# Two places more for raw weight pieces in block one of an attention and two-layer kernel

## The chip, the core and the metric

The kernel runs on one core of a Trainium2 chip. The metric is the time of one execution on the device, in microseconds (us); the median of several runs counts. TensorE (PE) multiplies matrices, VectorE (DVE), ScalarE (ACT) and GpSimd (POOL) work on elements, and SyncE (SP) issues all loads and stores of this kernel.

## The reference

```
def _attn_ref(q, k, v):                       # 4 batches, 8 heads, 576 tokens, 64 wide
    q_d, k_d, v_d = means over 4 neighbouring tokens
    out_d = sm_attn(q_d, k_d, v_d)             # softmax attention over the 144 pooled tokens
    out_up = np.repeat(out_d, factor, axis=2)
    mask = np.abs(pos[:, None] - pos[None, :]) < factor
    out_local = softmax(where(mask, q k^T / 8, -1e9)) v
    return (out_up + out_local).astype(np.float32)

x = attention output as (2304, 512)
h = x @ w_in;  x = relu(h)^2 @ w_out           # layer one: 512 -> 2048 -> 512, weights in float64
h = x @ w_in;  out = (h * cos(h)) @ w_out      # layer two, the same shapes, weights of its own
```

Matrix products of this precision are made of three parts: the weight is split into a high part and a low part of TensorE's fast 32-bit type, and so is the activation, and high x high, high x low and low x high are added.

## The kernel before, in words

The tokens are worked on as 40 windows of about 58 tokens; two windows are a `pair`. Layer one takes them in five blocks of eight windows (460 or 464 tokens). In block j, a loop over the 16 weight pieces f (128 of the 2048 hidden units each) makes stage A (`stage_a`, L808: 12 matmuls into the bank `ps_h`, of which there is one, from `xh`, `xl` and the weight's `w1hi` and `loa`), then on ScalarE `gt` (L832, L833) and its high part `gh` (L820), on VectorE the low part `gl` (L826), and stage B (`stage_b1`, L891: 12 matmuls into four `acc` banks). Stage A of a piece runs ahead of stage B of the piece before it.

The weights come as float64 in raw pieces of 1 MB. `conv1(f)` loads a piece (`load_raw`, L650, a tile named `raw`, of which there are two), and `split` makes a 32-bit float of it: a Prelu on ScalarE (L667) into a tile `bits` (two of them), a clamp (L671) and a shift (L674) on VectorE, and a join of the lower word (L676), which reads `raw` for the last time. Then ScalarE writes the high part `w1hi` (L687; 16 tiles `hi0` to `hi15`, one for each piece, which stay) and VectorE the low parts `loa` and `lob` (L697), which are also stored to `lo_d` (L726) and loaded again by later blocks (L734). So each of the 16 pieces of block one is converted just ahead of its use. Later the second layer's pieces pass through the same two raw tiles (`conv2`).

Ahead of block one there is a first phase: attention of the first batch's first eight windows. Its q and k (8 tiles), pooled values and value bands lie in tiles of weight high parts that are not in use yet: `spare` is the list of free ones, `kept` three that the value bands and a part of the pooled values take (`early_v`), `need` and `done` take and give back. One of the two raw tiles also holds pooled values in this phase. During block one, attention for block two is done beside the matmuls: pooling of the next batch (`pool`, loads `pl` at L264 and L267, sums at L368, L373, L375), its four `down` steps (scores L413, weights by GpSimd L424, transposes L434, values L450), and four `pair` steps (mask and scores L546 and L565, exponentials L387 or L398, transposes L504, values L607, the sum `xt` L624, and `xh` and `xl` at L636 and L638). When a block ends, its four banks are copied to a tile `y` (L929 on ScalarE, L931 on VectorE) and stored.

The program is written as generators, advanced in turn by a loop. A scheduling layer then sorts the instructions of each engine by a model of time; within an engine they run in that order. Places are handed out as the program is written: `used` and `caps` count tiles, and a generator goes on when a count allows it.

Of the kernel before, what the change touches and what calls it, by code (L numbers as in the profile page):

```python
# [8 lines left out]
F32 = mybir.dt.float32  # L9
F32R = mybir.dt.float32r  # L10
BF16 = mybir.dt.bfloat16
U32 = mybir.dt.uint32
AF = mybir.ActivationFunctionType
ALU = mybir.AluOpType
# [4 lines left out]
P = 128  # L19
# [12 lines left out]
DM = H * D  # L32
DFF = 2048
NK = DM // P
NF = DFF // P
# [10 lines left out]
AHEAD = 3  # L46
# [11 lines left out]
TOP_SCALE = 2.0 ** -112  # L58
TOP_ALPHA = 2.0 ** 32
TOP_MAX = (2.0 - 2.0 ** -3 - 2.0 ** -23) * 2.0 ** 16 * TOP_SCALE  # L60
LO_RING = (("loa", AHEAD), ("lob", AHEAD + LAG))
SPREAD = ("qk0", "pl", "dpr", "dpt")
LENT = {"dpr": "vw", "dpt": "pl"}
PRODUCTS = ((5, 5), (0, 0), (3, 6), (1, 1), (4, 4), (2, 2), (6, 3))
RANK = {"down": 0, "pair": 1, "pool": 2, "conv1": 3, "conv2": 3}
# [27 lines left out]
def kernel(  # L93
# [11 lines left out]
    nc = tc.nc  # L105
    weights = {1: w1.bitcast(U32), 2: w2.bitcast(U32)}
# [4 lines left out]
    wp = ctx.enter_context(tc.tile_pool(name="wp", bufs=1, side="right"))  # L111
# [19 lines left out]
    for t, v in zip(magic, (MAGIC, -MAGIC)):  # L131
# [9 lines left out]
    caps = {  # L141
        "a": 3, "h": 1, "acc": 4, "qkw": 2, "vw": 2, "pr": 4, "pt": 5, "xt": 2, "qp": 1, "xd": 2, "vp": 1, "av": 3, "pl": 2, "raw": 2,
        "dpr": 2, "dpt": 1, "qk0": 0,
    }
    used = dict.fromkeys(caps, 0)
# [5 lines left out]
    def need(name, n=1):  # L151
        while early[0] and name in SPREAD:
            if name not in ("qk0", "pl") and used[name] < caps[name]:
                used[name] += 1
                held.setdefault(name, []).append(None)
                return
            if spare:
                held.setdefault(name, []).append(spare.pop(0))
                return
            other = LENT.get(name)  # L160
            if other and used[other] < caps[other]:
                used[other] += 1
                held.setdefault(name, []).append(other)
                return
            yield
        while used[name] + n > caps[name]:
            yield
        used[name] += n

    def done(name, n=1):  # L170
        f = taken[name].pop(0) if early[0] and name in SPREAD else None
        if f is None:
            used[name] -= n
        elif f in caps:
            used[f] -= n
        else:
            spare.append(f)

    spare = list(range(AHEAD, NF))
    kept = [spare.pop() for _ in range(W0[1] // 4 + 1)]  # L180
    held, taken = {}, {}

# [465 lines left out]
    def load_raw(layer, f):  # L648
        raw = rawp.tile([P, 2 * DM, 2], U32, tag="raw", name="raw")
        nc.sync.dma_start(out=raw.rearrange("p c w -> p (c w)"), in_=weights[layer][f])  # L650
        return raw

    def behind(*names):
        for name in names:
            if name in last:
                return tc.issue_after(last[name])
        return nullcontext()
# [2 lines left out]
        return tc.issue_after(last["pe"]) if follows and not early[0] else nullcontext()  # L660

    def split(raw, hi, los=None, sums=None, held_back=None):
        low, top = raw[:, :, 0], raw[:, :, 1]
        x = rawp.tile([P, 2 * DM], U32, tag="bits", name="bits")
        xv = x.bitcast(F32)
        with behind("hi", "xh", "exp"):
            nc.scalar.activation(out=xv, in_=top.bitcast(F32), func=AF.Prelu, scale=TOP_SCALE, alpha=TOP_ALPHA)  # L667
        while held_back and held_back(0):
            yield
        with behind("pr" if early[0] and not added[0] else "gl", "xl"):  # L670
            nc.vector.tensor_scalar(  # L671
                out=xv, in0=xv, scalar1=TOP_MAX, scalar2=-TOP_MAX * TOP_ALPHA, op0=ALU.min, op1=ALU.max
            )
        nc.vector.tensor_scalar(out=x, in0=x, scalar1=3, scalar2=None, op0=ALU.logical_shift_left)  # L674
        yield
        joined = nc.vector.scalar_tensor_tensor(  # L676
            out=x, in0=low, scalar=29, in1=x, op0=ALU.logical_shift_right, op1=ALU.bitwise_or
        )
        if held_back and added[0] and "joined" not in last:
            last["xl"] = last["joined"] = joined.ins  # L680
        if sums:
            yield from sums(xv)
        yield "read"
        while held_back and held_back(1):
            yield
        with behind("hi", "xh", "xd"):
            nc.scalar.activation(out=hi, in_=xv, func=AF.Copy)  # L687
        yield
        while held_back and held_back(2):
            yield  # L690
        if los is None:
            nc.gpsimd.tensor_tensor(out=xv, in0=xv, in1=hi.bitcast(F32), op=ALU.subtract)
        else:
            for k, lo in enumerate(los()):
                cs = slice(k * DM, (k + 1) * DM)
                with behind("xl") if held_back else nullcontext():
                    nc.vector.tensor_tensor(out=lo, in0=xv[:, cs], in1=hi[:, cs].bitcast(F32), op=ALU.subtract)  # L697
        return xv
# [2 lines left out]
    lo1 = {}  # L701
    
    def conv1(f, after=0):
        yield from need("raw")
        raw = load_raw(1, f)
        yield
        yield
        while len(ready) < after or len(scored) < 4:
            yield
        hi1[f] = wp.tile([P, 2 * DM], F32R, tag=f"hi{f}", name=f"w1hi{f}")  # L710
        los = []

        def ring():
            los.extend(lop.tile([P, DM], F32R, tag=t, name=t, bufs=n) for t, n in LO_RING)
            return los

        waits = {0: lambda k: (divided[0], len(downs), len(ready))[k] < (W0[1], HPAIR, 6)[k], 1: lambda k: len(ready) < W0[1],
                 2: lambda k: k == 0 and "joined" not in last}
        for said in split(raw, hi1[f], ring, held_back=waits.get(f) if early[0] else None):
            if said:  # L720
                done("raw")
            yield
            while f == 2 and said and now[0] < 1:
                yield
        for k, lo in enumerate(los):
            nc.sync.dma_start(out=lo_d[f][:, k * DM:(k + 1) * DM], in_=lo.bitcast(F32))  # L726
            lo1[0, f, k] = lo
# [9 lines left out]
    def conv2(u):  # L737
        p, odd = divmod(u, 2)
        yield from need("raw")
        raw = load_raw(2, u)  # L740
        yield
        yield
        hi = rawp.tile([P, 2 * DM], F32R, tag="shi", name="shi", bufs=1)
        n = 3 * HALF
        rest = raw.rearrange("p c w -> p (c w)")
        total, top = rest[:, :n].bitcast(F32), rest[:, 2 * DM:2 * DM + n].bitcast(F32R)

        def sums(x):
            b11, b12, b21, b22 = (x[:, k * HALF:(k + 1) * HALF] for k in range(4))
            t1, t2, t3 = (total[:, k * HALF:(k + 1) * HALF] for k in range(3))  # L750
            with behind("gl", "xl"):
                nc.vector.tensor_tensor(out=t3, in0=b22, in1=b12, op=ALU.add)
            nc.vector.tensor_tensor(out=t1, in0=b12, in1=b11, op=ALU.subtract)
            yield
            with behind("gl", "xl"):
                nc.vector.tensor_tensor(out=t2, in0=t3, in1=b11, op=ALU.subtract)
            nc.vector.tensor_tensor(out=b12, in0=b21, in1=t2, op=ALU.subtract)
            yield

        steps, lo = split(raw, hi, sums=sums if odd else None), None  # L760
        while True:
            try:
                said = next(steps)
            except StopIteration as end:
                lo = end.value
                break
            if said and not odd:
                done("raw")
            yield
        if not odd:  # L770
            nc.sync.dma_start(out=wi_d[p][:, :2 * DM], in_=hi.bitcast(F32))
            nc.sync.dma_start(out=wi_d[p][:, 2 * DM:], in_=lo)
            return
        m = NPROD * HALF
        nc.sync.dma_start(out=wo_d[p][:, :2 * DM], in_=hi.bitcast(F32))
        nc.sync.dma_start(out=wo_d[p][:, m:m + 2 * DM], in_=lo)
        with behind("relu", "xh", "exp"):
            nc.scalar.activation(out=top, in_=total, func=AF.Copy)
        yield
        nc.gpsimd.tensor_tensor(out=total, in0=total, in1=top.bitcast(F32), op=ALU.subtract)  # L780
        yield
        nc.sync.dma_start(out=wo_d[p][:, 2 * DM:m], in_=top.bitcast(F32))
        nc.sync.dma_start(out=wo_d[p][:, m + 2 * DM:], in_=total)
        done("raw")
# [354 lines left out]
    for i in range(n1):  # L1139
        j, f = divmod(i, NF)  # L1140
# [40 lines left out]
    for i in range(n2 + 4):  # L1181
        j, p = divmod(i, NP2)
# [107 lines left out]
```

## Time and profile before

| | |
|---|---|
| median of 3 runs | 915.63 us (914.12 to 920.59) |
| profiled execution | 917.37 us |
| its span, first to last instruction | 915.6 us |
| TensorE busy | 892.2 us, 97% |
| VectorE busy | 644.6 us, 70% |
| ScalarE busy | 572.9 us, 63% |
| data moved | 223.55 MB, mean 244 GB/s |
| mean granted TensorE clock | 0.992 of full speed |

The profiled execution's own time lies a little above its span, since it counts what lies around the first and the last instruction. Times inside the profile are counted from the span's start.

### The profile page before, as it was taken

What the parts mean: (1) busy time and instruction counts of PE and PEld (TensorE: products, weight loads), DVE (VectorE), ACT (ScalarE), POOL (GpSimd) and SP (SyncE); (2) the same over time, 40 slices, a digit from 0 to 9 for tenths busy, and PEclk for the clock granted to TensorE, in tenths of its full rate; (3) what the DMA queues carried; (4) which work ended last, traced back from release to release, by engine and by line L of the source; (5) the groups of instructions that cost most, each with busy time, mean ns of one, the idle gap of its engine ahead of it and who ended that gap; (6) DMA issues with size and microseconds to landing.
All of it is one profiled execution on the core that took longest, in us unless ns stands there. A gap on an engine that the chain in (4) does not pass through costs nothing.

```text
span 915.6 us, 17788 instructions
## 1 busy us (share of the span) xinstructions
PE 892.2 (97%) x6950; PEld 812.8 (89%) x6950; DVE 644.6 (70%) x1266; ACT 572.9 (63%) x1039; POOL 93.1 (10%) x79
## 2 busy tenths in 40 slices
PE   7888999999999999999999999999999999999997
PEld 5667788888887888888998999999999999999997
DVE  7989987655775657553311188888888887888786
ACT  5678875455644555454534477677777677777774
POOL 2002110122303312221200000000000000000000
PEclk9899999999999999999999999999999999999999
DMA  9498878957898666884897966665666656566663
GB/s 296 166 320 301 300 284 301 326 209 257 300 331 281 253 234 220 299 313 162 285 393 245 345 233 195 206 193 185 201 206 197 201 198 199 192 193 206 207 229 104
DMA packets 72903, 223.55 MB, mean 244 GB/s; under 512 B 9620, under 2 KB 14612, under 8 KB 68724
## 3 DMA queue, kind: packets, MB, share of 16 engines
q1 hardware_dynamic: 72820, 222.43, 71.2%
q8 instruction: 54, 0.88, 0.4%
q14 instruction: 29, 0.24, 0.1%
HBM read 181.50 MB, written 40.89 MB: 243 GB/s over the span
## 4 chain that ended last, share of the span: by engine, by line
PE 86%; DMA 6%; DVE 5%; ACT 2%; issue 0%; DVEq 0%; ACTq 0%; SPq 0%
PE ps_h L843 22%; PE acc L915 19%; PE ps_h L808 19%; PE acc L891 18%; DMA pl<-in_pool_v_dram 3%; DMA pl<-in_pool_qk_dram 2%; PE ps_warm L1028 1%; PE ps_a L607 1%; PE ps_a L413 1%; PE ps_a L450 1%; DMA raw<-in_w_dram 1%; PE ps_a L565 1%; PE acc L913 1%; DVE vp L375 1%; PE ps_a L434 1%; PE ps_a L504 1%
## 5 line engine op out<-in xcount | busy, mean ns | idle before, releaser
L826 DVE TENSOR_TENSOR gl<-gt,gh 128x460 fp32r<-128x460 f32 (+1 forms) x80 | 58.8, 735 | 147.7 <-ACT gh L820 86.8
L843 PE MATMUL ps_h<-x,w2hi 128*128 128x256 f32 x1152 | 160.0, 281 | 0.0
L843 PEld LDWEIGHTS ps_h<-x,w2hi 128*128 128x128 f32 x1152 | 146.9, 188 | 0.1
L915 PE MATMUL acc<-bl,gh 128*128 128x256 f32 x504 | 140.6, 280 | 0.0
L808 PE MATMUL ps_h<-xh,w1hi 128*128 128x460 f32 (+1 forms) x320 | 123.0, 385 | 7.2 <-ACT gt L832 4.3
L891 PE MATMUL acc<-gl,w1hi 128*128 128x460 f32 (+1 forms) x320 | 120.9, 378 | 1.5 <-DVE gl L826 1.5
L808 PE MATMUL ps_h<-xl,w1hi 128*128 128x460 f32 (+1 forms) x320 | 119.9, 375 | 0.0
L832 ACT ACTIVATE gt<-ps_h 128x460 f32<-128x460 f32 (+1 forms) x80 | 44.2, 553 | 105.3 <-PE ps_h L808 105.2
L891 PE MATMUL acc<-gh,w1hi 128*128 128x460 f32 (+1 forms) x320 | 107.1, 374 | 0.0
L891 PE MATMUL acc<-gh,lo 128*128 128x460 f32 (+1 forms) x256 | 95.3, 372 | 0.0
L915 PEld LDWEIGHTS acc<-bl,gh 128*128 128x128 f32 x504 | 94.7, 188 | 0.0
L883 DVE TENSOR_TENSOR gl<-g,gh 128x896 fp32r<-128x896 f32 x72 | 78.2, 1086 | 11.0 <-ACT gh L878 11.0
L851 ACT ACTIVATE u<-ps_h,quarter 128x512 f32<-128x512 f32 x72 | 49.4, 686 | 52.2 <-PE ps_h L843 52.1
L915 PE MATMUL acc<-w2hi,gh 128*128 128x256 f32 x288 | 80.7, 280 | 0.0
L915 PE MATMUL acc<-w2hi,gl 128*128 128x256 f32 x288 | 80.2, 280 | 0.0
L858 DVE SCALAR_TENSOR_TENSOR r<-u,ps_h 128x512 f32<-128x512 f32 x72 | 49.4, 687 | 41.2 <-ACT u L853 40.4
L808 PEld LDWEIGHTS ps_h<-xh,w1hi 128*128 128x128 f32 x320 | 60.4, 189 | 17.0 <-ACT gt L832 5.0
L878 ACT ACTIVATE gh<-g 128x896 fp32r<-128x896 f32 x72 | 68.1, 946 | 10.4 <-DVE g L876 10.4
L863 ACT ACTIVATE r<-r,half_pi 128x512 f32<-128x512 f32 x72 | 51.8, 719 | 34.5 <-DVE r L859 34.5
L843 PE MATMUL ps_h<-x,w2lo 128*128 128x256 f32 x432 | 68.5, 280 | 0.0
L891 PEld LDWEIGHTS acc<-gl,w1hi 128*128 128x128 f32 x320 | 60.1, 188 | 9.2 <-DVE gl L826 2.6
L808 PE MATMUL ps_h<-xh,lo 128*128 128x460 f32 (+1 forms) x256 | 66.1, 377 | 0.0
(147 smaller groups left out, 1895.4 us busy)
## 6 DMA issues: line engine op xcount, KB each, us to landing
bl<-wo_d SPq DMA_DIRECT2D x70, 896.0 KB
raw<-in_w_dram SPq DMA_DIRECT2D x32, 1024.0 KB
lo<-lo_d SPq DMA_DIRECT2D x128, 256.0 KB
qkw<-in_win_qk_dram SPq DMA_DIRECT2D x16, 512.0 KB
pl<-in_pool_qk_dram SPq DMA_DIRECT2D x24, 288.0 KB
wo_d<-raw SPq DMA_DIRECT2D x16, 384.0 KB
out_dram<-o SPq DMA_DIRECT2D x18, 256.0 KB
vw<-in_win_v_dram SPq DMA_DIRECT2D x16, 256.0 KB
```

The source lines that it names most:

```text
L375: nc.vector.tensor_reduce(out=vp[:, i[0]:i[-1] + 1, hp * P:(hp + 1) * P], in_=t.rearrange("p (k j r) -> p k j r", k=len(i), r=FACTOR), op= ...
L808: nc.tensor.matmul(h[:, :n], a[:, c * P:(c + 1) * P], x[:, c, :n], start=i == 0, stop=i == len(order) - 1)
L826: last["gl"] = nc.vector.tensor_tensor(out=gl, in0=gt, in1=gh.bitcast(F32), op=ALU.subtract).ins
L832: last["relu"] = nc.scalar.activation(out=gt, in_=h, func=AF.Relu).ins
L843: nc.tensor.matmul(h[:, s * TB:(s + 1) * TB], a[:, c * P:(c + 1) * P], x[:, c], start=i == 0, stop=i == len(order) - 1,)
L851: nc.scalar.activation(out=u, in_=h, func=AF.Identity, bias=quarter, scale=float(1.0 / (2 * math.pi)))
L858: nc.vector.scalar_tensor_tensor(out=r, in0=u, scalar=-PI2_HI, in1=hv, op0=ALU.mult, op1=ALU.add)
L863: nc.scalar.activation(out=r, in_=r, func=AF.Sin, bias=half_pi, scale=1.0)
L878: nc.scalar.activation(out=gh, in_=g[:, 1:], func=AF.Copy)
L883: nc.vector.tensor_tensor(out=gl, in0=g[:, 1:], in1=gh.bitcast(F32), op=ALU.subtract)
L891: nc.tensor.matmul(acc[d][:, :n], a, x, start=f == 0 and i == 0, stop=f == NF - 1 and i == 2)
L915: nc.tensor.matmul(o, a[:, x], b, start=opens and i == 0, stop=p == NP2 - 1 and i == 2 and (k % 2 == 1 or k == NPROD - 1),)
```

## The change

Two pairs of high-part tiles, 12 to 15, become places for raw pieces in block one. `spare` is turned round, so that q and k of the first phase take the tiles 15 down to 8 (before: 3 to 10), and `kept` holds 3 to 5 (before: 15, 14, 13). When the first phase gives tiles 12 to 15 back, they go to a list `vacant` and not to `spare`. `conv1(f)` asks `raw_place` for a place: a raw tile if the count allows one, otherwise two vacant tiles of numbers above f. In the second case `load_spare` loads the piece as two halves of 512 KB. `split` works on a list of parts, so that the Prelu and the join run once for each half; the clamp, the shift and all later steps stay whole. After the join the two tiles return to `vacant`.

```diff
+NSPARE = 2
...
-            spare.append(f)
-
-    spare = list(range(AHEAD, NF))
+            (vacant if f >= NF - 2 * NSPARE else spare).append(f)
+
+    vacant = []
+    spare = list(range(NF - 1, AHEAD - 1, -1))
     kept = [spare.pop() for _ in range(W0[1] // 4 + 1)]
...
-        return raw
+        return [(slice(0, 2 * DM), raw)]
+
+    def load_spare(f, tags):
+        parts = []
+        for k, t in enumerate(tags):
+            cs = slice(k * DM, (k + 1) * DM)
+            raw = wp.tile([P, 2 * DM], F32R, tag=f"hi{t}", name="raw").bitcast(U32)
+            nc.sync.dma_start(out=raw, in_=weights[1][f][:, 2 * k * DM:2 * (k + 1) * DM])
+            parts.append((cs, raw.rearrange("p (c w) -> p c w", w=2)))
+        return parts
+
+    def raw_place(f):
+        while True:
+            if used["raw"] < caps["raw"]:
+                used["raw"] += 1
+                return ()
+            mine = [t for t in vacant if t > f]
+            if len(mine) > 1:
+                for t in mine[:2]:
+                    vacant.remove(t)
+                return mine[:2]
+            yield
...
-            nc.scalar.activation(out=xv, in_=top.bitcast(F32), func=AF.Prelu, scale=TOP_SCALE, alpha=TOP_ALPHA)
+            for cs, part in raw:
+                nc.scalar.activation(
+                    out=xv[:, cs], in_=part[:, :, 1].bitcast(F32), func=AF.Prelu, scale=TOP_SCALE, alpha=TOP_ALPHA
+                )
...
-        joined = nc.vector.scalar_tensor_tensor(
-            out=x, in0=low, scalar=29, in1=x, op0=ALU.logical_shift_right, op1=ALU.bitwise_or
-        )
+        for cs, part in raw:
+            joined = nc.vector.scalar_tensor_tensor(
+                out=x[:, cs], in0=part[:, :, 0], scalar=29, in1=x[:, cs], op0=ALU.logical_shift_right,
+                op1=ALU.bitwise_or,
+            )
...
-        yield from need("raw")
-        raw = load_raw(1, f)
+        tags = yield from raw_place(f)
+        raw = load_spare(f, tags) if tags else load_raw(1, f)
...
-            if said:
+            if said and tags:
+                vacant.extend(tags)
+            elif said:
                 done("raw")
```

Since the scheduling layer sorts anew, instructions move on every engine from the second piece of block one up to the first pieces of block two. Two places matter here.

SP's queue at the end of the first phase and the start of block one, before. Names are tiles; `raw` 128x2048 is a whole piece, `lo_d_99` and so on take the low parts of piece zero and the next ones.

```order
L513 DMA vw<-in_win_v_dram 128x512
L650 DMA raw<-in_w_dram 128x2048 x2
L726 DMA lo_d_99<-loa 128x512
L726 DMA lo_d_99<-lob 128x512
L650 DMA raw<-in_w_dram 128x2048
L524 DMA qkw<-in_win_qk_dram 128x1024
L264 DMA pl<-in_pool_qk_dram 128x576 x2
L726 DMA lo_d_100<-loa 128x512
L726 DMA lo_d_100<-lob 128x512
L650 DMA raw<-in_w_dram 128x2048
L264 DMA pl<-in_pool_qk_dram 128x576
```

The same place now, with the changed kernel's line numbers (L660 loads a half, L652 a whole piece, L755 stores low parts).

```order
L515 DMA vw<-in_win_v_dram 128x512
L660 DMA raw<-in_w_dram 128x1024 x4
L652 DMA raw<-in_w_dram 128x2048 x2
L755 DMA lo_d_99<-loa 128x512
L755 DMA lo_d_99<-lob 128x512
L660 DMA raw<-in_w_dram 128x1024 x2
L526 DMA qkw<-in_win_qk_dram 128x1024
L266 DMA pl<-in_pool_qk_dram 128x576 x2
L755 DMA lo_d_100<-loa 128x512
L755 DMA lo_d_100<-lob 128x512
L266 DMA pl<-in_pool_qk_dram 128x576 x2
```

Four halves (pieces one and two) and two whole pieces (three and four) stand ahead of the first low-part store, where two whole pieces (one and two) stood; piece five follows as halves. From piece six on every piece is loaded whole.

ScalarE's order where block one ends, before. `ps_h_2028` is stage A of block one's last piece, `ps_h_2123` that of block two's first one, `ps_h_2210` of its second; `acc_887` and `acc_889` are banks of block one's result.

```order
L636 ACTIVATE xh<-xt 128x4x112
L832 ACTIVATE gt<-ps_h_2028 128x460
L833 ACTIVATE gt<-gt 128x460
L820 ACTIVATE gh<-gt 128x460
L506 COPY pt<-ps_a 128x256
L371 COPY qp<-qc 64x144 x2
L398 ACTIVATE pr<-pr 128x256 x2
L832 ACTIVATE gt<-ps_h_2123 128x460
L833 ACTIVATE gt<-gt 128x460
L820 ACTIVATE gh<-gt 128x460
L929 COPY y<-acc_887 128x460
L929 COPY y<-acc_889 128x460
```

The same place now; `ps_h_2135` is block two's first stage A and `ps_h_2222` its second, `acc_903` and `acc_905` the banks.

```order
L638 ACTIVATE xh<-xt 128x4x116
L958 COPY y<-acc_903 128x460
L958 COPY y<-acc_905 128x460
L508 COPY pt<-ps_a 128x256
L638 ACTIVATE xh<-xt 128x4x112
L508 COPY pt<-ps_a 128x256
L400 ACTIVATE pr<-pr 128x256 x2
L861 ACTIVATE gt<-ps_h_2135 128x460
L862 ACTIVATE gt<-gt 128x460
L849 ACTIVATE gh<-gt 128x460
L861 ACTIVATE gt<-ps_h_2222 128x460
```

The copies of block one's result now stand ahead of the last `xh` of block two's input (128x4x112) and ahead of block two's first `gt`; before, they stood behind both. On VectorE the copies of the two other banks stand ahead of the last `xl` in the same way, and TensorE has all of block one's stage B ahead of block two's first stage A, and then block two's second stage A right behind the first.

## Rows read from the trace of the kernel before

**Rows 1.** The page, part 1: busy us of each engine (share of the span), instructions.

```profile
PE 892.2 (97%) x6950; PEld 812.8 (89%) x6950; DVE 644.6 (70%) x1266; ACT 572.9 (63%) x1039; POOL 93.1 (10%) x79
```

**Rows 2.** Busy time by stretch: its length, engines, granted clock, DMA share, GB/s.

```profile
32.00:36.00 4.00, 3.44 (x40) 2.70 (x40) 3.54 (x8) 1.82 (x6) 0.00 (x0) 1.00 0.00 0
42.00:52.00 10.00, 7.33 (x48) 5.47 (x48) 9.89 (x17) 4.80 (x9) 0.00 (x0) 1.00 0.60 205
48.00:105.00 57.00, 51.63 (x353) 40.99 (x354) 51.03 (x103) 44.09 (x127) 9.17 (x9) 1.00 0.90 316
105.00:160.00 55.00, 55.00 (x463) 46.00 (x461) 46.30 (x93) 38.89 (x89) 5.06 (x7) 1.00 0.85 295
```

**Rows 3.** SP's queue in order of time: start, duration, line, load.

```profile
27.70 8.33 SPq L650 DMA_DIRECT2D raw<-in_w_dram  x2
...
59.88 0.33 SPq L650 DMA_DIRECT2D raw<-in_w_dram  x1
```

**Rows 4.** ScalarE in order of time: three Prelus; in brackets idle before, and releaser.

```profile
43.96 1.18 ACT L667 ACTIVATE bits<-raw 128x1024 f32<-128x1024 f32 x1 [1.96 <-DVE lob L697]
...
51.56 1.15 ACT L667 ACTIVATE bits<-raw 128x1024 f32<-128x1024 f32 x1 [1.80 <-DMA raw<-in_w_dram]
...
67.03 1.13 ACT L667 ACTIVATE bits<-raw 128x1024 f32<-128x1024 f32 x1 [3.86 <-DMA raw<-in_w_dram]
```

**Rows 5.** TensorE's waits from 36 to 105 us: total us, times, longest.

```profile
PE ps_h L808 <- ACT gt L832: 2.3, 1, 2.3
PE ps_h L808 <- ACT w1hi L687: 1.7, 3, 1.0
PE acc L891 <- DVE gl L826: 1.5, 2, 0.9
PE ps_h L808 <- ACT xh L636: 1.1, 1, 1.1
PE ps_a L434 <- POOL dpr L424: 0.9, 1, 0.9
PE ps_a L413 <- ACT dpt L441: 0.5, 1, 0.5
PE ps_a L434 <- ACT dpr L387: 0.3, 1, 0.3
PE ps_a L450 <- ACT dpt L441: 0.2, 1, 0.2
```

**Rows 6.** VectorE in order of time: a join, a low part, a pooling sum.

```profile
45.25 1.23 DVE L676 SCALAR_TENSOR_TENSOR bits<-raw,bits 128x1024 uint32<-128x1024 uint32 x1
...
49.25 0.68 DVE L697 TENSOR_TENSOR loa<-bits,w1hi 128x512 fp32r<-128x512 f32 x1
...
54.84 0.75 DVE L368 TENSOR_REDUCE qc<-pl 128x144 f32<-128x576 f32 x1 [1.40 <-DMA pl<-in_pool_qk_dram]
```

**Rows 7.** Busy time by stretch, the first loads.

```profile
6.00:8.00 2.00, 2.00 (x9) 0.83 (x8) 1.08 (x2) 0.30 (x1) 0.00 (x0) 1.00 1.02 364
```

**Rows 8.** DMA issues: engine, count, KB of each.

```profile
qk<-in_pool_qk_dram SPq DMA_DIRECT2D x8, 288.0 KB
```

**Rows 9.** VectorE in order of time: the last xl of block two's input.

```profile
148.53 0.63 DVE L638 TENSOR_TENSOR xl<-xt,xh 128x448 fp32r<-128x448 f32 x1 [0.65 <-ACT xh L636]
```

**Rows 10.** The chain that ended last, around the end of block one.

```profile
150.06 0.22 PE ps_a L504 x2
...
150.99 2.71 PE ps_h L808 x12
153.69 4.59 PE acc L891 x22
```

**Rows 11.** The same chain after 281 us.

```profile
281.69 0.55 ACT gt L832
...
282.28 4.35 PE ps_h L808 x12
```

**Rows 12.** Busy time by stretch, the same place.

```profile
280.00:285.00 5.00, 3.02 (x11) 2.35 (x10) 4.11 (x11) 3.60 (x7) 2.18 (x2) 0.80 0.97 368
```

More of the change, by code (lines that the diff above doesn't have):

```diff
@@ L662, in split @@
     def split(raw, hi, los=None, sums=None, held_back=None):
-        low, top = raw[:, :, 0], raw[:, :, 1]
         x = rawp.tile([P, 2 * DM], U32, tag="bits", name="bits")
@@ L744, in conv2 @@
         n = 3 * HALF
-        rest = raw.rearrange("p c w -> p (c w)")
+        rest = raw[0][1].rearrange("p c w -> p (c w)")
         total, top = rest[:, :n].bitcast(F32), rest[:, 2 * DM:2 * DM + n].bitcast(F32R)
```

## The prediction

> **What bounds the kernel now.** I read the page's busy shares first, then the busy time by stretch, then the waits of TensorE, and last the engines behind these waits. TensorE is busy for 892.2 of 915.6 us [rows 1], so a change of loads can win at most the 23 us in which it is not, and only in the stretch where loads are late. From 105 to 160 us TensorE has no gap at all, while from 48 to 105 us, the first nine or ten pieces of block one, it is busy for 51.63 of 57.00 us [rows 2]: 5.37 us of idle time. This is the stretch of the change. In it the DMA engines are busy to 0.90, VectorE for 51.03 us, ScalarE for 44.09 us. Earlier, from 32 to 36 us, nothing is loaded at all (share 0.00) [rows 2].
>
> The queue shows why loads are late there. Pieces one and two (counted from zero) are issued in one row that begins at 27.70 us and lasts 8.33 us, to 36 us, because piece two has to wait until piece zero has been read; piece five is issued at 59.88 us, when piece three has been read [rows 3]. Its first reader, the Prelu of line 667, starts at 67.03 us, after ScalarE stood 3.86 us for this load; the Prelu at 51.56 us stood 1.80 us in the same way [rows 4]. But the Prelu at 43.96 us waited 1.96 us for VectorE's low part, through the two `bits` tiles [rows 4]: no weight load is late there.
>
> How much of this reaches TensorE is in its list of waits from 36 to 105 us [rows 5]. Two of them end before 48 us and have nothing to do with loads: 1.1 us for the block's input (xh) and 2.3 us for gt, the first block-one evacuation, which stands behind a conversion on ScalarE. After 48 us there are 1.7 us for w1hi (three waits), 1.5 us for gl (two: 0.9 and, by difference, 0.6), and 0.9 + 0.5 + 0.3 + 0.2 = 1.9 us for the pooled attention's steps. Together 5.1 of the 5.37 us.
>
> **The change, part by part.** *Two places more.* Pieces one and two no longer wait for a raw tile: their four halves are issued once the scores of the first phase are read, behind the last vw load of the first phase; piece three then takes the tile of the pooled values (27.70 us), piece four that of piece zero (36 us) [rows 3]. So by 40 us five pieces have been asked for, not three: 2 MB move out of the full stretch into one in which the engines stand still. At 316 GB/s [rows 2] that is 6.6 us of queue time fewer between 48 and 105 us. Piece five reuses the halves of piece one. From piece six on everything is in the two old places: the lead of two pieces passes on, but is not renewed from piece eight.
>
> *What goes.* The waits for w1hi, 1.7 us, are those behind late raw pieces and go. Of gl's 1.5 us, the longer one of 0.9, at the first gl, stays: VectorE has next to no gap before it, 9.89 of the 10 us from 42 to 52 [rows 2]. The other 0.6 goes: VectorE stood 1.40 us for a pooled piece at 54.84 us [rows 6], queued behind a raw load. The 1.9 us of the attention's steps come from a VectorE that runs late after such waits; I let them go as well. Sum: 1.7 + 0.6 + 1.9 = 4.2 us. Bounds: 1.7, if only weight waits go, and 5.37.
>
> *What halves cost.* Three pieces take two Prelus and two joins in place of one. A join of 1024 columns takes 1.23 us, an operation of 512 columns 0.68 us [rows 6], so two halves cost 2 x 0.68 - 1.23 = 0.13 us more. Pieces one and two lie in the stretch where VectorE has no gap: 0.26 us. Piece five hides behind TensorE's work. The Prelus hide in ScalarE's idle time there (12.9 of 57 us). SP issues three loads more; behind them stand the lo stores and the pool loads, and SP has gaps of microseconds between rows [rows 3]. The eight loads of q and k of 288 KB at the start moved 364 GB/s with the engines full [rows 7, 8], so I charge halves of 512 KB nothing. The Trainium skill ("DMA: Bandwidth & Descriptors", "Anatomy of one DMA — SWDGE (gpsimd) path") gives each transfer a fixed part of about 2.0 us beside its bytes, measured on another issue path; charged in full for piece five, whose second half falls into the full queue, the sum below would be 2.0 us worse, about -0.6 in place of -2.6 us; the row with 364 GB/s does not bear it out.
>
> *The order of first-phase tiles.* q and k take tiles 15 down to 8, the value bands and one pooled piece tiles 3 to 5. Their readers belong to the first phase, which is over when block one begins at 42 us; piece three, the first to take one of the three, is converted from 51.56 us on [rows 4]. No cost.
>
> *The end of block one.* The engines' order is made anew, and here is the price. On ScalarE the two copies of block one's result (y) now stand ahead of the last x of block two and ahead of the first gt of block two; before, one more gt stood between. Since these copies need the last matmuls of block one, block two's first matmul now starts only when block one is finished, with no rest of it left to fill. Before, the last xl was written at 148.53 us [rows 9], block two's first 12 matmuls ran at 150.99 us and 22 matmuls of block one (4.59 us) followed them as cover [rows 10]. Without it the chain of add, xh and xl, each taken at the 0.63 us of xl [rows 9], 1.9 us, is covered only by transposes and scores, 0.93 us (150.06 to 150.99) and two more transposes of 0.22 [rows 10]: 1.15 us. 0.75 us stay open. Then block two's second group waits for the single ps_h bank, an evacuation of 0.55 us [rows 11], with nothing beside it. Together 1.3 us. Bounds: 0, if attention is early, and 5.7, see the slower rival.
>
> *Sum.* -4.2 + 0.26 + 1.3 = -2.6 us. The profiled execution took 917.37 us, its span 915.6, so 1.8 us lie around it; the median of the three runs is 915.63 us, 0.2% below the profiled one. I take the difference to the median: 915.6 - 2.6 = 913.0 us.
>
> **The rivals.** *Slower: the drain at the end of block one costs the clock.* After 280 us TensorE stands for 2.0 us behind a late gt (busy 3.02 of 5.00 us), the granted clock has a mean of 0.80 there [rows 12], and the next 12 matmuls take 4.35 us [rows 11], against 2.71 us for the 12 at 150.99 us [rows 10]: 1.64 us more, at the lower level of 1.2 GHz for most of them. If attention for block two is not faster (its steps lie on VectorE and GpSimd and only partly behind loads), the drain becomes that case: 1.9 us uncovered, two groups of 12 at the low level (3.3 us), the evacuation 0.55: 5.7 us. With only the w1hi waits gone, -1.7 + 0.26 + 5.7 = +4.3, so 919.9 us. It decides when TensorE stands some 2 us there. For it: the new order itself. Against it: the 2.3 us wait near 46 us [rows 5] left the clock at 1.00 [rows 2], and pools and scores get their loads earlier too.
>
> *The change does not do what it says.* VectorE is the engine that delays TensorE, with 51.03 of 57 us busy, and early pieces just wait for it; the gain of 1.7 us goes into halves and drain. Change about 0, 915.5 us. For it: the `bits` wait at 43.96 us. Against: VectorE itself stood for loads [rows 6].
>
> *More gain.* All 5.37 us go and attention is early enough that nothing drains: 915.6 - 5.4 = 910.2. If then also the stall at 280 us is hit differently, since all transfers come earlier against it, its 2.0 + 1.64 us go: 906.6. For it: the stall hangs on loads of pooled values one after another. Against it: the order of instructions there is unchanged.
>
> **How the numbers follow.** Forecast, -1 to -4.5 us: 0.50, time 913.0. More gain: 0.20. No effect, within 1 us: 0.14. Slower rival: 0.16. A change under 1% (9.2 us) can hardly be told from none by these three runs, which spread from 914.12 to 920.59. The forecast, the rival without effect, most of the gains and nearly all of the losses lie inside it. The range goes from 908, the gain with part of the later stall, to 919.5, most of the slower rival: I leave out about 0.1 below and 0.07 above. Faster by over 1% needs nearly all of both gains: 0.06; slower by over 1% needs twice the slower rival's drain: 0.03; within 1%: 0.91.
>
> **What would show it.** In the changed profile the halves should be issued between 22 and 28 us and the DMA share of 32 to 36 us should be well above 0. The Prelus of pieces three and five should not wait for loads, and TensorE's w1hi waits between 48 and 105 us should be gone, its idle time there between 1 and 2 us; if they stay behind gl or dpr, VectorE is the bound. The waits of 2.3 and 1.1 us before 48 us should stand as they are. About 150 us a new gap of some 1.3 us should stand ahead of block two. If this gap is over 2 us and the granted clock there under 1.00, the slower rival holds. The forecast is wrong in its mechanism if TensorE's idle time of 48 to 105 us stays above 4 us, or if the time moves in stretches after 300 us.

## The result, and the profile after

The changed kernel takes 924.02 us (median of 12 runs, 919.80 to 929.34), the kernel before, beside it, 917.61 us (12 runs): a ratio of 1.0072 with an interval of 1.0048 to 1.0097, so 6.4 us slower, where 2.6 us less were forecast. The profiled executions lie further apart: 926.37 us with a span of 924.6 us, against 917.37 and 915.6.

The page of the changed kernel, part 1 (busy us, share, instructions), stands against [rows 1]:

```profile
PE 894.9 (97%) x6950; PEld 815.1 (88%) x6950; DVE 645.0 (70%) x1269; ACT 573.5 (62%) x1042; POOL 95.6 (10%) x79
```

TensorE stands for 924.6 - 894.9 = 29.7 us, before for 23.4: 6.3 of the 9.0 us of span. The other 2.7 us are matmuls that took longer. The busy time by stretch (columns as in [rows 2]) says where:

```profile
32.00:36.00 4.00, 3.00 (x34) 2.25 (x34) 3.90 (x10) 2.01 (x7) 0.00 (x0) 1.00 0.63 257
48.00:57.00 9.00, 8.20 (x31) 7.05 (x32) 6.10 (x13) 6.67 (x18) 0.00 (x0) 0.81 0.83 274
48.00:105.00 57.00, 48.37 (x310) 40.50 (x311) 48.20 (x98) 40.91 (x114) 6.04 (x7) 0.91 0.81 269
89.00:105.00 16.00, 11.67 (x80) 9.81 (x79) 11.78 (x27) 11.89 (x40) 3.09 (x3) 0.79 0.83 272
155.00:182.00 27.00, 24.88 (x268) 20.27 (x267) 14.55 (x33) 12.14 (x25) 1.19 (x2) 1.00 0.81 277
```

The loads do what the change says: from 32 to 36 us the DMA share is 0.63, not 0.00, and from 48 to 105 us it has fallen from 0.90 to 0.81 [rows 2]. Yet TensorE's idle time in that stretch has risen from 5.37 to 8.63 us, VectorE and ScalarE are less busy as well, and the granted clock has a mean of 0.91. (0.7 us of the rise is no new stop: the wait for gt, 2.3 us before and 2.4 us now, ends at 48.80 and not at 48.06 us, and so falls into the stretch.) From 155 to 182 us 2.12 us are idle, where TensorE had no gap at all before.

TensorE's waits from 36 to 105 us, against [rows 5]:

```profile
PE ps_a L548 <- ACT dpr L389: 3.7, 1, 3.7
PE ps_h L837 <- ACT gt L861: 2.4, 1, 2.4
PE ps_h L837 <- DVE loa L724: 1.9, 1, 1.9
PE ps_h L837 <- ACT xh L638: 1.2, 1, 1.2
PE acc L920 <- DVE gl L855: 1.0, 1, 1.0
PE ps_a L415 <- ACT pr L389: 0.5, 1, 0.5
PE ps_h L837 <- ACT w1hi L714: 0.4, 1, 0.4
```

The waits for w1hi are down from 1.7 to 0.4 us, as forecast. Two that were not there before, of 3.7 and 1.9 us, outweigh them. In this profile both lead to an instruction that waits for a load in front of work that was ready. VectorE in order of time, at the shorter one:

```profile
57.13 0.75 DVE L370 TENSOR_REDUCE qc<-pl 128x144 f32<-128x576 f32 x1 [3.03 <-DMA pl<-in_pool_qk_dram]
57.91 0.75 DVE L375 TENSOR_REDUCE kp<-pl 128x144 f32<-128x576 f32 x1
58.58 0.68 DVE L724 TENSOR_TENSOR loa<-bits,w1hi 128x512 fp32r<-128x512 f32 x1
```

A pooling sum stands 3.03 us for its load, and the low part of piece two, for which TensorE waits, is queued behind it. The old order has the same sum ahead of the same low part, and there TensorE does not wait for it. Before, the sum stood 1.40 us, at 54.84 us [rows 6], and the low part came next:

```profile
55.51 0.68 DVE L697 TENSOR_TENSOR loa<-bits,w1hi 128x512 fp32r<-128x512 f32 x1
```

New are the second sum between the two (0.67 us) and a load that came later. ScalarE in order of time, at the longer stop:

```profile
91.42 1.12 ACT L690 ACTIVATE bits<-raw 128x1024 f32<-128x1024 f32 x1 [4.50 <-DMA raw<-in_w_dram]
92.44 0.37 ACT L389 ACTIVATE dpr<-ps_a,dmx 96x144 f32<-96x144 f32 x1
```

The Prelu of piece eight, loaded into one of the two old places, stands 4.50 us for that load, and the exponentials of the pooled attention behind it hold a bank that TensorE's next scores need. SP issued the load at 82.92 us:

```profile
82.92 0.35 SPq L652 DMA_DIRECT2D raw<-in_w_dram  x1
```

What the stop does to the matmuls behind it (TensorE in order of time):

```profile
93.67 0.42 PE L548 MATMUL ps_a<-const_b 64*64 64x256 bf16 x2 [3.71 <-ACT dpr L389]
...
95.33 0.75 PE L837 MATMUL ps_h<-xh,w1hi 128*128 128x460 f32 x1
95.88 0.59 PE L837 MATMUL ps_h<-xl,w1hi 128*128 128x460 f32 x1
96.26 0.59 PE L837 MATMUL ps_h<-xh,w1hi 128*128 128x460 f32 x1
96.64 0.59 PE L837 MATMUL ps_h<-xl,w1hi 128*128 128x460 f32 x1
```

They follow each other after 0.38 us. At 85 us, ahead of the stop, the same matmuls did so after 0.21:

```profile
85.08 0.37 PE L837 MATMUL ps_h<-xl,w1hi 128*128 128x460 f32 x1
85.28 0.37 PE L837 MATMUL ps_h<-xh,w1hi 128*128 128x460 f32 x1
85.49 0.37 PE L837 MATMUL ps_h<-xl,w1hi 128*128 128x460 f32 x1
```

The granted clock is at its lower level, 1.2 of 2.4 GHz, from 93 to 100 us, and also from 49 to 52 us behind the wait of 2.4 us for gt.

Two readings are left. **Theory O:** the order is what costs. The scheduling layer has put many rows elsewhere (a row is one instruction in an engine's order), all between about 45 and 185 us, and engines that keep their order now stand in front of late loads with ready work behind. How many rows depends on the way of counting: the expectations below say some 550 matmul, 210 VectorE and 140 ScalarE rows; the fewest whose move turns one order into the other, by line and shape, are 141, 73 and 53. **Theory L:** the loads cost. A pooled load is queued behind the halves of piece five, and from piece six on the look-ahead is back at two places.

### The profile page after: what moved, and what is told of

It is laid out like the page before. It is cut to its first block, busy times and chain, and to the rows that moved or that the text cites. A ratio compares the mean times of both kernels' runs of the same rounds, so it can differ in the third digit from the quotient of the medians.

```text
span 924.6 us, 17794 instructions
## 1 busy us (share of the span) xinstructions
PE 894.9 (97%) x6950; PEld 815.1 (88%) x6950; DVE 645.0 (70%) x1269; ACT 573.5 (62%) x1042; POOL 95.6 (10%) x79
## 4 chain that ended last, share of the span: by engine, by line
PE 85%; DMA 7%; DVE 6%; ACT 2%; issue 0%; SPq 0%; DVEq 0%; ACTq 0%
PE ps_h L872 22%; PE acc L944 19%; PE ps_h L837 18%; PE acc L920 18%; DMA pl<-in_pool_v_dram 4%; DMA pl<-in_pool_qk_dram 2%; PE ps_warm L1057 1%; DMA raw<-in_w_dram 1%; PE ps_a L452 1%; PE ps_a L415 1%; PE ps_a L609 1%; PE ps_a L567 1%; PE ps_a L436 1%; PE acc L942 1%; DVE bits L702 1%; DVE vp L377 1%
## 5 line engine op out<-in xcount | busy, mean ns | idle before, releaser
L837 PEld LDWEIGHTS ps_h<-xl,w1hi 128*128 128x128 f32 x320 | 61.3, 192 | 7.7 <-DVE xl L640 1.6
```

Source lines behind the costliest of these rows:

```text
L837: nc.tensor.matmul(h[:, :n], a[:, c * P:(c + 1) * P], x[:, c, :n], start=i == 0, stop=i == len(order) - 1)
```

## The experiments

**Loads and order taken apart.** The order of all matmuls, VectorE and ScalarE instructions can be written out and tied, with edges that set the order alone. Each row is named by its line and its number among the rows of that line; the halves stand where the whole Prelu and join stood. Tied to its own order, the kernel before keeps every row in its place on every engine, so the tie itself moves nothing. SP's queue is not tied. In the two runs that follow it came out, but for the weight pieces and two other loads, as in the kernel whose order is tied, so "order" takes in the order of the pooled loads and of the low parts on SP. No run tells the two apart.

```diff
...
+    for name, said in ORDER.items():
+        chain = []
+        for run in said.split():
+            line, _, span = run.partition(":")
+            a, _, b = span.partition("-")
+            chain += [at[name, int(line), k] for k in range(int(a), int(b or a) + 1)]
+        for one, two in zip(chain, chain[1:]):
+            tc.add_manual_dep(
+                two, one.name, mybir.DependencyInfo(mybir.DependencyClass.NoSync, mybir.DependencyReason.DATA),
+                reason="the other kernel's order",
+            )
```

*New loads, old order:*

> The changed kernel with all its loads (two more places, halves, piece five in the halves of piece one), but the matmuls, the VectorE and the ScalarE instructions each stand in the order of the kernel before, tied by order-only edges. Theory O (the loss is the new order: between about 45 and 185 us some 550 matmul, 210 VectorE and 140 ScalarE rows stand elsewhere, and attention steps and weight steps get in each other's way): the loss of 6 to 9 us goes; time from 4 us below to 1 us above the kernel before, TensorE idle for at most 5.4 us from 48 to 105 us, no stop of 3.7 us at 90 us, no half clock after 48 us, and the forecast of -2.6 us can be seen or not. Theory L (the loss is the loads: a pooled load queued behind the halves, look-ahead back to two places from piece six): still 4 to 9 us slower than before, with stops behind a load.

Measured: 918.81 us beside 918.11, ratio 1.0006 (0.9987 to 1.0025). *Old loads, new order:*

> The kernel before with its loads, but matmuls, VectorE and ScalarE instructions in the order of the changed kernel. Theory O: 4 to 9 us slower than before, with stops of TensorE at about 57 and 90 us and a half clock behind them. Theory L: within 1.5 us of before. A third reading, that the new order is right for the new loads and wrong for the old ones, would show as more than 9 us.

Measured: 926.20 us beside 918.11, ratio 1.0088 (1.0057 to 1.0119). Old loads in the new order are as slow as the changed kernel, new loads in the old order as fast as the kernel before. Theory O is shown, with SP's order as part of it; L falls. (The third reading expected over 9 us; by the ratio it is 8.1, with 5.2 to 10.9 allowed, so a small share of it is not excluded.) The stretches agree. New loads, old order (48 to 105 us and 155 to 182 us; columns as above):

```profile
48.00:105.00 57.00, 53.33 (x358) 43.12 (x359) 52.78 (x109) 46.05 (x131) 9.97 (x9) 0.97 0.84 282
...
155.00:182.00 27.00, 27.00 (x221) 23.07 (x220) 16.15 (x33) 12.72 (x23) 3.70 (x5) 1.00 0.92 319
```

Old loads, new order:

```profile
48.00:105.00 57.00, 47.18 (x308) 39.08 (x308) 48.53 (x95) 40.13 (x112) 9.78 (x7) 0.94 0.85 291
105.00:155.00 50.00, 48.43 (x348) 38.93 (x347) 39.78 (x78) 35.12 (x87) 9.95 (x8) 1.00 0.84 279
155.00:182.00 27.00, 25.21 (x269) 20.57 (x268) 14.04 (x32) 12.16 (x26) 1.19 (x2) 1.00 0.83 280
```

In the first, the idle time of 48 to 105 us is 3.67 us, 1.7 less than before, and there is none at the end of block one. (Its clock is at the lower level from 49 to 52 us, and the waits of 1.5 us for gl that before has [rows 5] do not occur behind these longer matmuls; a run with the full clock there follows below.) In the second it is 9.82 us, more than in the changed kernel, and the stops around 160 to 180 us are there with the old loads too. The stops are not at the same places in all details (here TensorE waits 3.1 us for w1hi and 2.3 us for GpSimd's pr, not for loa and dpr): the new order meets whichever load is late.

**An order made anew without other loads.** Only pieces one, two and five are written in halves, with the old loads:

```diff
...
-            nc.scalar.activation(out=xv, in_=top.bitcast(F32), func=AF.Prelu, scale=TOP_SCALE, alpha=TOP_ALPHA)
+            for cs in cut:
+                nc.scalar.activation(
+                    out=xv[:, cs], in_=top[:, cs].bitcast(F32), func=AF.Prelu, scale=TOP_SCALE, alpha=TOP_ALPHA
+                )
...
+        cut = [slice(k * DM, (k + 1) * DM) for k in range(2)] if f in (1, 2, 5) else (slice(0, 2 * DM),)
```

The join likewise.

> The kernel before with its loads, in which only the Prelu and the joining instruction of pieces one, two and five are written as two halves each; the scheduler then moves some 345 matmul, 150 VectorE and 110 ScalarE rows of block one. Theory O: the time moves by several us in either direction (between -5 and +9), not by the 0.3 us that six short instructions more cost. Theory L: within 1 us of before.

Measured: 922.12 us beside 918.11, ratio 1.0029 (1.0009 to 1.0049), 2.7 us by the ratio. Three joins in halves cost little. In its profile two halves take 1.28 or 1.29 us together, where a whole join takes 1.22 or 1.23, some 0.2 us for all three:

```profile
45.48 1.29 DVE L680 SCALAR_TENSOR_TENSOR bits<-raw,bits 128x512 uint32<-128x512 uint32 x2
...
51.08 1.28 DVE L680 SCALAR_TENSOR_TENSOR bits<-raw,bits 128x512 uint32<-128x512 uint32 x2
...
58.90 1.22 DVE L680 SCALAR_TENSOR_TENSOR bits<-raw,bits 128x1024 uint32<-128x1024 uint32 x1
```

The rest comes with the order: TensorE's idle time of 48 to 105 us is 8.61 us (busy 48.39). A second and a third new order:

```diff
-        start_at(f - AHEAD - 1, conv1, f)
+        start_at(f - AHEAD - 3, conv1, f)
```

> The changed kernel, in which every piece of block one from the third on may ask for a place two slots earlier, so that the two more places go on being used. Theory L in its form that the look-ahead falls back to two places from piece six: 3 to 6 us faster than the changed kernel, so 0 to 4 us slower than before. Theory O: the order is another one again, and the time does not follow the loads: anywhere from 3 us faster to 9 us slower than before, with stops behind instructions of VectorE and ScalarE and not behind loads.

Measured: 923.36 us beside 918.11, ratio 1.0050 (1.0031 to 1.0068). The look-ahead does not fall back now, and in the profile 48 to 105 us are better (busy 52.60 us), but 3.1 us are idle from 105 to 155 and 2.1 from 155 to 182 us.

```diff
-NSPARE = 2
+NSPARE = 1
```

> The changed kernel with one place more instead of two, in its own order, which the scheduler makes anew: some 500 matmul, 200 VectorE and 150 ScalarE rows stand elsewhere than before. Theory O: the new order costs here too, 2 to 9 us slower than before, although fewer loads move. If the loss follows the loads, it is about half of that of two places: 3 to 4 us slower.

Measured: 923.85 us beside 918.03, ratio 1.0074 (1.0049 to 1.0098). One place more costs as much as two. The loss does not follow the loads.

**The tiles alone.** `NSPARE = 0`: the list is turned round, no row moves.

> The kernel before with only the list of spare tiles turned round: q and k of the first phase take the last tiles, the bands of v the first free ones, no place more. No row moves on any engine, only a few instructions wait for another tile's reader. Theory O: within 1 us of before. If the tiles themselves cost (first pieces wait for the tiles of the v bands): 1 to 3 us slower, with a stop of TensorE between 45 and 60 us that before does not have.

Measured: 916.57 us beside 918.03, ratio 0.9983 (0.9963 to 1.0002). No cost, as the prediction said of this part.

**Where in the order.** The tied order is cut at the first matmul of piece eight.

> The new loads; up to piece eight (its first matmul, some 100 us) the order of the kernel before, from there the rows that are left in the order of the changed kernel. If the loss lies in both stretches (stops and half clock from 48 to 105 us, and stops of 2.1 us together from 155 to 182 us): 2 to 3 us slower than before, with the stops at 160 to 180 us still there. If all of it lies before 105 us: within 1.5 us of before.

Measured: 922.84 us beside 918.03, ratio 1.0063 (1.0041 to 1.0084).

> The new loads; up to piece eight the order of the changed kernel, from there the rows that are left in the order of the kernel before. If the loss lies in both stretches: 3 to 5 us slower than before, no stop from 155 to 182 us. If all of it lies before 105 us: 6 to 8 us slower.

Measured: 922.40 us beside 918.03, ratio 1.0053 (1.0032 to 1.0074). Both stretches cost. The profiles agree; first old, then new:

```profile
48.00:105.00 57.00, 52.32 (x354) 42.35 (x354) 52.82 (x108) 43.92 (x123) 9.93 (x9) 1.00 0.86 289
...
155.00:182.00 27.00, 24.03 (x241) 20.05 (x241) 14.61 (x31) 11.66 (x22) 1.25 (x3) 1.00 0.80 262
```

First new, then old:

```profile
48.00:105.00 57.00, 49.97 (x333) 41.14 (x334) 51.62 (x105) 44.75 (x126) 10.43 (x9) 0.93 0.86 297
...
155.00:182.00 27.00, 27.00 (x236) 23.28 (x229) 18.29 (x38) 13.22 (x25) 3.11 (x3) 1.00 0.93 315
```

The idle time stands in the stretch that has the new order. The late part costs more than the 2 to 3 us expected of it. By the ratios the two losses are 5.8 and 4.9 us, 10.7 together, where the whole new order costs 6.6; with some 2 us of uncertainty on each of the three it stays open whether they add.

The run with the new order first has the changed kernel's loads, and its rows at the two stops of the result in the same order. In its profile the stop at the low part of piece two is 0.25 us, not 1.91, and the one at piece eight's Prelu 0.83, not 3.71:

```profile
58.05 1.10 PE L837 MATMUL ps_h<-xh,loa 128*128 128x460 f32 x4 [0.25 <-DVE loa L724]
...
88.54 0.30 PE L548 MATMUL ps_a<-const_b 64*64 64x256 bf16 x2 [0.83 <-ACT dpr L389]
```

So the length of these two stops changes from one execution to the next, and one profile does not give their price. What the order costs is known from the medians.

**Single rows.** The changed kernel's own order, tied, with one ScalarE row moved (given here by the order's rows and not as code):

```diff
-ACT L690 Prelu of piece eight
 ACT L389 dpr (three exponentials)
 ACT L508 pt
 ACT L714 w1hi of piece seven
+ACT L690 Prelu of piece eight
```

> The changed kernel with its own order of matmuls, VectorE and ScalarE instructions tied down, and one ScalarE row moved: the Prelu of piece eight, which stood 4.50 us for its load at 91.42 us ahead of three exponentials of the pooled attention, now stands behind them and behind the conversion of piece seven. Theory O, in the form that single rows in the wrong place make the loss: the stop of 3.7 us at 90 us and the half clock behind it go, 4 to 7 us faster than the changed kernel (0 to 3 us slower than before). If the loss there only moves to piece eight: 0 to 2 us faster than the changed kernel. Theory that piece eight's late load itself is what costs: no gain.

Measured: 925.21 us beside 917.50, ratio 1.0085 (1.0057 to 1.0113): nothing gained. Its profile shows the stop of 3.7 us gone and the clock at 1.00 from 89 to 105 us, but TensorE's waits from 84 to 105 us are now:

```profile
PE ps_h L837 <- ACT gt L861: 1.6, 1, 1.6
PE ps_a L436 <- POOL dpr L426: 0.7, 1, 0.7
PE acc L920 <- DVE gl L855: 0.4, 1, 0.4
PE ps_a L548 <- ACT dpr L389: 0.3, 1, 0.3
```

In this profile part of the stop moved to the next rows, and 1.01 us more is idle from 105 to 155 us. Then also, on VectorE, the two low parts of piece two and the shift between them (L724, L699, L724) ahead of the sum that stood 3.03 us:

> As the kernel with the Prelu of piece eight moved, and on VectorE the two low parts of piece two and the shift between them stand ahead of the pooled sums that waited 3.03 us for their load at 57.13 us. Theory O: the stop of 1.9 us at 57 us goes, 1 to 2 us faster than with the one row moved. If the weights' wait is only replaced by a later one: no difference.

Measured: 921.19 us beside 917.50, ratio 1.0042 (1.0022 to 1.0062): some 4 us better than with one row, where 1 to 2 were expected. Why is not shown: the profile with one row moved has no stop at that low part to begin with (TensorE has no wait for loa there). Nor is a gain over the changed kernel clear: 2.8 us by the ratios, with some 3 us of uncertainty. That single rows make the loss is thus argued and not shown; what is shown is that the order as a whole does.

**Is there more to win?** Loads two slots earlier, in the old order:

> Pieces may ask for a place two slots earlier, in the halves and the two old places, and matmuls, VectorE and ScalarE rows stand in the order of the kernel before. In the run with the new loads in the old order only 0.6 us of TensorE's waits from 48 to 105 us were left for weights, so still earlier loads can give 0 to 0.6 us more: within 1 us of that run. If loads are still what bounds there: 1 to 3 us faster than it.

Measured: 916.75 us beside 917.50, ratio 0.9990 (0.9975 to 1.0004). Not to be told from before; this and the turned-round tiles are the lowest medians, and neither beats it for certain. In its profile the clock is at 1.00 from 48 to 105 us, so it shows what the loads alone do there: TensorE waits 0.6 us for w1hi (before 1.7), 1.5 for gl (1.5), and 0.9 and 0.5 for the pooled attention's dpr and dpt (1.9 in all). Since its matmuls, those of the new loads in the old order and those of before stand in one order, the time from block one's first matmul to block two's first can be compared. Before, new loads in the old order, and loads two slots earlier:

```profile
42.06 0.48 PE L808 MATMUL ps_h<-xh,w1hi 128*128 128x460 f32 x1 [1.14 <-ACT xh L636]
...
150.91 0.48 PE L808 MATMUL ps_h<-xh,w1hi 128*128 128x460 f32 x1
```

```profile
43.01 0.48 PE L837 MATMUL ps_h<-xh,w1hi 128*128 128x460 f32 x1 [1.24 <-ACT xh L638]
...
150.06 0.48 PE L837 MATMUL ps_h<-xh,w1hi 128*128 128x460 f32 x1
```

```profile
42.12 0.48 PE L837 MATMUL ps_h<-xh,w1hi 128*128 128x460 f32 x1 [1.25 <-ACT xh L638]
...
149.50 0.48 PE L837 MATMUL ps_h<-xh,w1hi 128*128 128x460 f32 x1
```

That is 108.85, 107.05 and 107.38 us. In these profiles the new loads gain 1.8 us in block one, and the loads two slots earlier 1.5; the medians are too uncertain to show it. New loads, old order, and two ScalarE rows moved:

```diff
-ACT L714 w1hi of piece one
 ACT L861 gt of piece zero
+ACT L714 w1hi of piece one
...
-ACT L400 pr (one exponential)
 ACT L861 gt at 281 us
+ACT L400 pr (one exponential)
```

> New loads, old order, and two ScalarE rows moved: the first evacuation of block one (gt) ahead of the conversion of piece one, and the one at 281 us ahead of an exponential that stands behind a late pooled sum on VectorE. The stop of 2.1 us at 281 us and its half clock (eight matmuls some 0.38 us apart, not 0.21) go, 3.4 us; at 49 us 0.5 us, and 1.4 us more if the clock then stays up. So 3.5 to 5.5 us faster than new loads in the old order, 913 to 915 us where before takes 918. If the stop at 281 us only moves to the next row: within 1.5 us of it.

Measured: 919.01 us beside 917.50, ratio 1.0009 (0.9991 to 1.0028). The expectation fell. At block one's first evacuation TensorE now stands 1.98 us for w1hi, where it stood 2.42 for gt. At 281 us the stop behind gt is gone, and TensorE stands as long a few rows on, for the exponentials that were passed, which GpSimd scales first:

```profile
287.45 0.69 PE L506 MATMUL ps_a<-const_sb,pr 128*128 128x128 f32 x2 [2.21 <-POOL pr L494]
```

## Why the prediction was wrong

- *The loads:* right. Four halves are issued from 23.41 us, the DMA share of 32 to 36 us is 0.63, the waits for w1hi are 0.4 us.
- *What goes, -4.2 us:* this is the step that failed. It took the stops behind loads away and left every other row of 48 to 105 us where it was, although the order is made anew there; only the end of block one was read for that, as "the price". The idle time rose by 3.3 us instead, to 8.63, over the 4 us that the prediction named as the sign of a wrong mechanism. The order as a whole costs 6.6 us by the ratio, or 8.1 with the old loads. With the order held, the loads take 1.8 and 1.5 us off block one in two profiles, near the term's lower bound of 1.7. The 1.9 us of the pooled attention, "I let them go as well", stayed for the most part: TensorE waits 1.0 us for dpr and 0.5 for dpt with the new loads in the old order, 0.9 and 0.5 with loads two slots earlier.
- *With the order held, is the sum right?* Not shown to be: 918.81 beside 918.11 us allows from 1.2 us gained to 2.3 lost, two slots earlier from 2.3 gained to 0.4 lost. The 2.6 us lie outside both.
- *Halves, +0.26 us:* about twice too much. Two halves of a join take 1.29 us together and a whole one 1.23, so 0.06 us for each piece and not 0.13; a single half takes 0.69 us, but the second starts before the first has ended. As an edit left to the sorter, halves alone cost 2.7 us, since they move rows.
- *The tiles' order, 0:* right.
- *The end of block one, +1.3 us:* there is a new loss, of the kind described (a gt with nothing beside it, 0.64 and 0.63 us, and the sum xt, 0.64 and 0.20 us), 2.12 us of stops, later than said (160 to 180 us, not 150). The sum had 1.3. It belongs to the order, not to the loads, as the term said: with the old loads it is 1.79 us, with the old order none.
- *The clock:* priced only in the slower rival, at about 150 us. There it stays at 1.00. It fell at 49 and 93 us, at 49 with the new loads in the old order too. The note that the 2.3 us wait near 46 us left the clock at 1.00 held for one profile and not for others (below).
- *The slower rival* came nearest in time (919.9 us), but by the wrong place. The rival "VectorE-bound" falls: VectorE is less busy there, 48.20 us, and stands for loads. The stop at 280 us did not go: from 290 to 297 us TensorE is busy for 4.81 of 7.00 us, the same stop some 9 us later, without the half clock.

Standing and clock can be told apart roughly over all runs: each has its span and its mean granted clock, and the span times that mean is an estimate of the time at full clock. Its median is 911.0 us for the changed kernel (12 runs) and 907.3 for the one before (the 76 runs beside the experiments), so by this estimate 3.7 us of the 6.4 are standing. The mean clock is 0.9875 against 0.9901, and 0.0026 of 920 us is 2.4 us: most of the rest. The same estimate gives 908.3 us for the new loads in the old order, 913.6 for the old loads in the new order, and 910.9 for the run with two rows moved, as much as for the changed kernel: by this estimate, what that run gained lies in the clock.

## What to carry to other kernels

Where a scheduling layer sorts, an edit has two effects, what it does and the order that it causes; four edits here (the change, the halves alone, two slots earlier, one place more) were left to the sorter, and each made the kernel 2.7 to 6.8 us slower, whatever it did to the loads. Tie the old order and run the edit in it: that separates the two in one run. When reading a new order ahead of a run, look on each in-order engine for every instruction that waits for a load, and name what stands behind it; and do not credit a row's move with its whole stop: here the next rows stood nearly as long, and the same stop was 3.71 us in one profile and 0.83 in another.

## What was not expected of the hardware

The granted clock behind the stop at 46 to 49 us differs with the same stop. In all fourteen profiles the clock is at the lower level from about 20 us on, in the first phase, and rises again. In the seven where it was back at 1.00 by 31 us (before; halves alone; two slots earlier in either order; old then new order; turned-round tiles; one place more) it stayed there through the stop; in the six where it came back between 31 and 37 us, the next stop of some 2.4 us was followed by 3 to 4 us at half clock, and in the one where it came back at 45 us the stop of 2.0 us at 50 us was too. New loads in the old order and two slots earlier in the old order have their matmuls in the same order and stand on different sides (48 to 57 us, columns as above):

```profile
48.00:57.00 9.00, 7.92 (x30) 6.80 (x31) 7.68 (x17) 6.58 (x16) 0.00 (x0) 0.81 0.86 299
```

```profile
48.00:57.00 9.00, 7.57 (x33) 6.05 (x34) 7.18 (x15) 7.76 (x24) 0.00 (x0) 1.00 0.99 363
```

What sets the first return was not tried.
